# v's loads issued one a score step, the first duo read in 1024-byte pieces by two queues, the last bank emptied behind the first weights

## The chip, the core and the metric

The kernel runs on one core of one Trainium2 chip. TensorE (PE, with its weight loads as PEld), VectorE (DVE), ScalarE (ACT), GpSimd (POOL) and SyncE (SP) each work through a list of their own, in order, and wait for each other by semaphores. Matrix products land in PSUM banks, which DVE and ACT empty into SBUF. The metric is device time in microseconds of one execution.

## What is computed

Three stages stand behind each other: sigmoid attention over 4 batches of 12 heads (448 rows of 64), whose output is x of 1792 rows by 768, and then two mixtures of eight experts, each of which sends a row to one expert.

```python
scores = scale * np.matmul(q, k.transpose(0, 1, 3, 2)) - np.log(S)
attn_out = np.matmul(1.0 / (1.0 + np.exp(-scores)), v)
x = attn_out.transpose(0, 2, 1, 3).reshape(B * S, H * D)
# first mixture, for rows with x @ w_skip > 0; e_idx = argmax(x @ w_gate)
y[mask] = gate_w[mask, None] * (np.maximum(x[mask] @ w1[e], 0.0) @ w2[e])
# second mixture: e_idx = argmax of the normed x against normed expert rows, over tau
out[mask] = gate_w[mask, None] * (np.maximum(x[mask] @ w1[e], 0.0) @ w2[e])
```

## The kernel before

**Attention** (function `attention`) goes by duos: twelve groups of four heads, three to a batch. A duo has seven score steps, one for each 64 rows of k. In a step PE makes four products of 64x64 by 448 into a pair of banks `psS` (`score`, L589; the trace counts each as two matmuls), ACT turns the pair into `A` by one sigmoid (L593), and two steps later four products with v add into the two banks `psO` of the duo (`av`, L607). `psS` has two pairs, so the score of step h+2 waits for the sigmoid of step h. g counts steps over all duos; w is the duo and h the step in it.

**A duo's end** falls into step h=1 of the next duo: after the last `av`, `take_x` empties the two `psO` banks into `xT`, one on DVE (L524, two copies) and one on ACT (L522, two copies). At h=2 no `av` runs, at h=3 two do, the first of which needs the emptied banks.

**Loads.** `load_qk` reads k and q of the duo after next with eight DMAs of 112 KB on SP's queue, at h=0; `turn` transposes them on DVE (L580) at h=3 and h=4 of the duo before their use. `load_v` reads v of the next duo with four DMAs of 112 KB on ACT's queue, all at h=2, so on ACT they stand behind the two copies of `take_x` and ahead of the next sigmoid. Each DMA on SP's or ACT's queue takes the next of eight completion semaphores, and is issued only when the DMA that had it last has landed.

**The first duo** is read by `load_first` on SP with eight DMAs of 256-byte pieces, and `turn_first` transposes it on PE, four transposes of 112 rows by 128 columns for each of four halves (L572), into one bank each, emptied by DVE (L576) or ACT (L574).

**The steps beside attention.** A list of small steps runs one at a time beside the score steps. After a batch's last duo, router steps s1, s2 and s3 follow; each puts a few matmuls on PE. After the third batch (its last `av` is at h=1 of duo 9, and `at` counts steps from there) further steps follow by the table `at`: `gates` (two ACT operations, five on DVE, L336 to L340), `plan_first` (ten on DVE, L360 to L369, which write `pa`), `start` (reads `pa` into registers of ACT, DVE and SP, and loads the first weights), `gate_cols` (DVE, L347 to L678, which write `G`), `rows` (one product of `G` on PE into `ps_G`, L684), and seven steps of `split_gated` (ACT L697, DVE L695 and L698).

**Behind attention**, `split_unit` splits the first expert's weights into a high part h (ACT, L756) and a low part l (DVE, L757), and `dense` multiplies (L766 and L767 with h, L768 with l). The second of the two last `psO` banks is emptied between the first three pieces of this split and the rest; the first is emptied ahead of it.

Of the kernel before, what the change touches and what calls it, by code (L numbers as in the profile page):

```python
# [10 lines left out]
F32 = mybir.dt.float32  # L11
F32R = mybir.dt.float32r
I32 = mybir.dt.int32
AF = mybir.ActivationFunctionType
# [7 lines left out]
def sigmoid_attention_moe_moe_kernel(  # L22
# [15 lines left out]
    nc = tc.nc  # L38
    B, H, S, D = q.shape
    NE, DM, DF = w1.shape  # L40
    NT = B * S
    P = 112
    C = S // P
    NP = H // 2
# [20 lines left out]
    def bank(name):  # L65
        if not BANKS:
            return psA.tile([128, 512], F32, tag="psA", name=name)
        turn[0] ^= 1
        return BANKS[turn[0]]
# [10 lines left out]
    ident = const("ident", [128, 128])  # L80
    make_identity(nc, ident)
    bias = const("bias", [128, 1])
    nc.vector.memset(bias, 0.0)
    nc.scalar.activation(bias, bias, AF.Sigmoid)
    nc.vector.memset(bias, -math.log(S))
    xT = const("xT", [128, ND, NT])


# [437 lines left out]
    def attention():  # L526


        with ExitStack() as a:
# [5 lines left out]

            def load_first():

                t = LDU[0] = {nm: ld.tile([P, 2, C, 2 * D], F32, tag=nm + "0", name=nm + "0", bufs=1) for nm in "kq"}
                for i in range(2):
                    for nm, src in (("k", k), ("q", q)):  # L540
                        for j in range(2):
                            nc.sync.dma_start(
                                t[nm][:, i, :, j * D : (j + 1) * D], src[0, i + 2 * j].rearrange("(c p) d -> p c d", c=C)
                            )

            def load_qk(w):

# [7 lines left out]
                            src[b, h : h + 2, :, f : f + 32].rearrange("i (t r) d -> r (i t) d", r=32),  # L555
                        )

            def load_v(w):
                b, d = duos[w]
                t = LDU[w]["v"] = ld.tile([128, 2, NH, D], F32, tag="v", name="v")  # L560
                for i in range(2):
                    for j in range(2):
                        nc.scalar.dma_start(
                            t[KT * i : KT * i + KT, j], v[b, 4 * d + i + 2 * j].rearrange("(h r) d -> r h d", r=KT)
                        )

            def turn_first(nm, i):
                if i == 0:
                    ST[0, nm] = wk.tile([128, 2, S], F32, tag=nm + "T", name=nm + "T")
                ps = bank("ps_t")  # L570
                for c in range(C):
                    nc.tensor.transpose(ps[:, c * P : (c + 1) * P], LDU[0][nm][:, i, c], ident[:P, :P])  # L572
                if i:
                    nc.scalar.activation(ST[0, nm][:, i], ps[:, :S], AF.Copy)  # L574
                else:
                    nc.vector.tensor_copy(ST[0, nm][:, i], ps[:, :S])  # L576

            def turn(w, nm):
                dst = ST[w, nm] = wk.tile([128, 2, S], F32, tag=nm + "T", name=nm + "T")
# [16 lines left out]
            def av(w, h):  # L596
                t = LDU[w]["v"]
                b, d = duos[w]
                if h == 0:
                    ST[w, "o"] = [  # L600
                        bank("psO") if w == N - 1 and i else psO.tile([128, 512], F32, tag="psO", name="psO") for i in range(2)
                    ]
                at = ST.pop((w, "a", h))
                for i in range(2):
                    r = slice(KT * i, KT * i + KT)
                    for j in range(2):
                        nc.tensor.matmul(  # L607
                            ST[w, "o"][i][D * j : D * j + D, :S], lhsT=t[r, j, h, :], rhs=at[r, j, :],
                            start=h == 0, stop=h == NH - 1,
                        )  # L610
                if h == NH - 1:
                    for i in range(2):
                        if w < N - 1 or not i:
                            take_x(b, d, i, ST[w, "o"][i])

            N = len(duos)
            G, LAG = N * NH, 2
            load_first()
            load_v(0)
            for i in range(2):  # L620
                turn_first("k", i)
                turn_first("q", i)
            load_qk(1)
            load_v(1)
            load_qk(2)
            todo = setup_steps(wk)
            late = {}
            for g in range(G + LAG):
                w, h = divmod(g, NH)
                if 0 < w < N - 2 and h == 0:  # L630
                    load_qk(w + 2)
                if w > 0 and w + 1 < N and h == LAG:
                    load_v(w + 1)
                if g < G:
                    score(w, h)
                if w + 1 < N and h in (3, 4):
                    turn(w + 1, "kq"[h - 3])
                for r in {LAG: (), LAG + 1: (LAG + 1, LAG)}.get(h, (LAG,)):
# [6 lines left out]
                if done % NH == 0 and done > 0:  # L645
                    b, d = duos[done // NH - 1]
                    if d == NP // 2 - 1 and b < B - 1:
                        assert not todo
                        s1, s2, s3 = route_stages(R1, b, x_of(b))
                        todo = [None, s1, s2, None, s3]  # L650
                        if b == B - 2:
                            fs = [s1, s2, s3, lambda: gates(R1, 0, B - 1), lambda: plan_first(R1)] + first_steps()
                            at = [g + i for i in (2, 3, 5, 5, 7, 8, 8, 10, 10, 11, 14, 15, 16, 17)] + [G]
                            todo, late = [], schedule({}, fs, at)
            return ST[N - 1, "o"][1]

    R1, R2 = Route(0), Route(1)
    FIRST = {}
# [571 lines left out]
    NB = {}  # L1230
    for f in split_unit(0)[:3]:
        f()
    take_x(B - 1, NP // 2 - 1, 1, last_x)
    for f in split_unit(0)[3:]:
        f()
    na = nc.values_load(K["pa"][0:1, 0:1], min_val=0, max_val=1)
# [187 lines left out]
```

## Time and profile before

| what | us |
|---|---|
| median of three runs | 607.29 (606.9 to 608.69) |
| the profiled execution | 605.65 |
| its span, first to last instruction | 603.9 |
| PE busy in it | 572.8 |
| first score product on PE | 12.69 |
| first product with v | 18.66 |
| first expert product (L766) | 163.60 |

The profile is of one execution. Times in its views count from the span's start; 1.75 us of the execution lie outside the span. A row of the timeline gives start, duration, engine, line, operation, tiles and count; in brackets stands how long the engine was idle before it and what ended that. A q behind an engine's name means its queue or sequencer, as for the issue of a DMA.

### The profile page before, as it was taken

The page shows a single profiled execution, that of the slowest core. Times are in us where ns is not written, and L with a number is a line of the kernel's source. Part 1 is how long each engine was busy: PE and PEld are TensorE (multiplying, and loading weights), DVE is VectorE, ACT ScalarE, POOL GpSimd, SP SyncE. Part 2 cuts the span into 40 slices and gives each one's busy share as a digit, 9 for nine tenths or more (in the row PEclk, how much of TensorE's full clock was granted, in tenths as well). Part 3 has the DMA queues.
Part 4 walks back from the last instruction along what each step waited for, and adds up shares of the span by engine and source line. Part 5 has one row for each costly group of instructions (what it writes and reads, how often), then busy time and mean ns, then how long its engine had stood idle before and what let it go on. Part 6 is the DMA issues. An engine that isn't in the chain of part 4 may idle for free. (4 is left out here: it accounts for less than half of the span.)

```text
span 603.9 us, 9912 instructions
## 1 busy us (share of the span) xinstructions
PE 572.8 (95%) x3706; PEld 426.5 (71%) x3706; DVE 302.9 (50%) x762; ACT 274.3 (45%) x445; POOL 7.5 (1%) x15
## 2 busy tenths in 40 slices
PE   4999999999999999999969999999999999999994
PEld 2333334333389898997849899979998899898882
DVE  0452325237657679572147773577456674541222
ACT  1766675666932374342027423653248322532111
POOL 2010000000000000000000000000000000000000
PEclk9999999999999999999999999999999999999998
DMA  9989987963350504331538032260509050553343
GB/s 140 132 125 124 112 109 101 140 99 105 136 201 9 195 19 158 106 104 54 187 135 291 24 117 92 85 216 4 206 1 298 3 209 1 160 194 104 117 146 99
DMA packets 142618, 73.35 MB, mean 121 GB/s; under 512 B 107506, under 2 KB 132550, under 8 KB 142544
## 3 DMA queue, kind: packets, MB, share of 16 engines
q1 hardware_dynamic: 119616, 66.40, 43.1%
q10 hardware_dynamic: 22736, 5.97, 4.8%
q8 instruction: 38, 0.62, 0.4%
q14 instruction: 36, 0.29, 0.2%
q0 software_dynamic: 192, 0.07, 0.1%
HBM read 66.90 MB, written 5.70 MB: 120 GB/s over the span
## 5 line engine op out<-in xcount | busy, mean ns | idle before, releaser
L766 PE MATMUL bank<-xs,h 128*128 128x448 f32 x288 | 108.2, 376 | 5.7 <-DVEq L1268 5.0
L766 PE MATMUL y<-hh,h 128*128 128x448 f32 x288 | 108.5, 377 | 0.0
L786 ACT ACTIVATE hh<-bank 128x448 fp32r<-128x448 f32 x48 | 26.0, 542 | 178.7 <-PE bank L768 166.4
L768 PE MATMUL bank<-xs,l 128*128 128x448 f32 x288 | 105.6, 367 | 1.4 <-DVE l L757 1.4
L767 PE MATMUL bank<-xs,h 128*128 128x448 f32 x288 | 106.0, 368 | 0.0
L767 PE MATMUL y<-hl,h 128*128 128x448 f32 x288 | 105.6, 367 | 0.0
L768 PE MATMUL y<-hh,l 128*128 128x448 f32 x288 | 105.6, 367 | 0.0
L593 ACT ACTIVATE A<-psS,bias 128x896 f32<-128x896 f32 x84 | 83.5, 1006 | 46.5 <-PE psS L589 31.7
L757 DVE TENSOR_TENSOR l<-r,h 128x512 fp32r<-128x512 f32 (+1 forms) x115 | 85.3, 792 | 4.6 <-ACT h L756 3.0
L787 DVE SCALAR_TENSOR_TENSOR hl<-bank,hh 128x448 fp32r<-128x448 f32 x48 | 29.9, 623 | 114.5 <-ACT hh L786 114.1
L589 PE MATMUL psS<-qT,kT 64*64 64x448 f32 x672 | 79.6, 555 | 4.4 <-ACT A L593 4.3
L607 PE MATMUL psO<-A,v 64*64 64x448 f32 x672 | 78.0, 539 | 0.9 <-DVE xT L524 0.9
L756 ACT ACTIVATE h<-r 128x512 fp32r<-128x512 f32 (+1 forms) x115 | 74.6, 710 | 0.4 <-DMA r<-in_moe_w_dram 0.3
L766 PEld LDWEIGHTS bank<-xs,h 128*128 128x128 f32 x288 | 54.4, 189 | 15.2 <-issue 6.2
L766 PEld LDWEIGHTS y<-hh,h 128*128 128x128 f32 x288 | 54.1, 188 | 8.2 <-issue 2.9
L768 PEld LDWEIGHTS bank<-xs,l 128*128 128x128 f32 x288 | 54.4, 189 | 6.6 <-DVE l L757 1.7
L767 PEld LDWEIGHTS bank<-xs,h 128*128 128x128 f32 x288 | 54.5, 189 | 4.3
L768 PEld LDWEIGHTS y<-hh,l 128*128 128x128 f32 x288 | 54.1, 188 | 4.9
L767 PEld LDWEIGHTS y<-hl,h 128*128 128x128 f32 x288 | 54.2, 188 | 4.6 <-issue 0.2
L589 PEld LDWEIGHTS psS<-qT,kT 64*64 64x64 f32 x672 | 24.0, 135 | 45.2 <-issue 24.8
L607 PEld LDWEIGHTS psO<-A,v 64*64 64x64 f32 x672 | 28.7, 133 | 38.1 <-issue 27.5
L524 DVE COPY xT<-psO 64x448 f32<-64x448 f32 x24 | 14.8, 619 | 50.3 <-PE psO L607 50.1
(250 smaller groups left out, 444.3 us busy)
## 6 DMA issues: line engine op xcount, KB each, us to landing
r<-in_moe_w_dram SPq DMA_DIRECT2D x62, 768.0 KB, 6.0
k<-in_k_dram SPq DMA_DIRECT2D x48, 112.0 KB, 3.8
v<-in_v_dram ACTq DMA_DIRECT2D x48, 112.0 KB, 3.0
q<-in_q_dram SPq DMA_DIRECT2D x48, 112.0 KB, 3.9
out_dram<-row SPq DMA_DIRECT2D x3, 1344.0 KB, 6.7
out_dram<-row SPq DMA_DIRECT2D x1, 896.0 KB, 5.2
stg<-in_moe_w_dram SPq DMA_DIRECT2D x1, 768.0 KB, 7.3
row<-in_moe_w_dram SPq DMA_DIRECT2D x1, 768.0 KB, 8.8
```

Of the source, the lines that this page charges most:

```text
L524: nc.vector.tensor_copy(x, ps[64 * j : 64 * j + 64, :S])
L589: nc.tensor.matmul(ps[KT * i : KT * i + KT, j, :S], lhsT=kT[r, i, h * KT : (h + 1) * KT], rhs=qT[r, i], start=True, stop=True,)
L593: nc.scalar.activation(at, ps[:, :, :S], AF.Sigmoid, bias=bias, scale=1.0 / math.sqrt(D))
L607: nc.tensor.matmul(ST[w, "o"][i][D * j : D * j + D, :S], lhsT=t[r, j, h, :], rhs=at[r, j, :], start=h == 0, stop=h == NH - 1,)
L756: nc.scalar.activation(dst_h, src, AF.Copy)
L757: nc.vector.tensor_sub(dst_l, src, dst_h.bitcast(F32))
L766: nc.tensor.matmul(ps, lhsT=ah, rhs=bh, start=first, stop=False)
L767: nc.tensor.matmul(ps, lhsT=ah, rhs=bl, start=False, stop=False)
L768: nc.tensor.matmul(ps, lhsT=al, rhs=bh, start=False, stop=last)
L786: nc.scalar.activation(a, ps[:, :S], AF.Relu)
L787: nc.vector.scalar_tensor_tensor(l, ps[:, :S], 0.0, a.bitcast(F32), op0=ALU.max, op1=ALU.subtract)
```

## The change

- `load_v` takes a list of parts, and the loop calls it with one part a step, at h=2 to h=5, behind `score`. Duo 1's v, loaded ahead of the loop before, goes the same way in duo 0.
- `load_first` issues four DMAs of 224 KB instead of eight, k on SP and q on ACT, in pieces of 1024 bytes: a partition holds four rows in a row of the sequence (p c) instead of rows 112 apart (c p). `turn_first` makes eight transposes of 112 by 64 instead of four of 112 by 128 for each half, four to each bank of a `psS` pair, and both DVE and ACT empty one bank each, reordering the columns.
- The sigmoid on `bias`, which brings ACT's table load, and the memset behind it move from the kernel's head behind `load_first`.
- Both last `psO` banks are emptied behind the first three pieces of `split_unit`.
- The table `at` puts `gates` three steps later, `plan_first` one, `start` two, `gate_cols` three, and the others one or two later.

```diff
@@ const bias @@
     nc.vector.memset(bias, 0.0)
-    nc.scalar.activation(bias, bias, AF.Sigmoid)
-    nc.vector.memset(bias, -math.log(S))
@@ load_first @@
-                t = LDU[0] = {nm: ld.tile([P, 2, C, 2 * D], F32, tag=nm + "0", name=nm + "0", bufs=1) for nm in "kq"}
+                t = LDU[0] = {nm: ld.tile([P, 2, 2, C * D], F32, tag=nm + "0", name=nm + "0", bufs=1) for nm in "kq"}
                 for i in range(2):
-                    for nm, src in (("k", k), ("q", q)):
-                        for j in range(2):
-                            nc.sync.dma_start(
-                                t[nm][:, i, :, j * D : (j + 1) * D], src[0, i + 2 * j].rearrange("(c p) d -> p c d", c=C)
-                            )
+                    for nm, src, queue in (("k", k, nc.sync), ("q", q, nc.scalar)):
+                        queue.dma_start(
+                            t[nm][:, i], src[0, 0:4].rearrange("(j i) (p c) d -> p i j (c d)", i=2, c=C)[:, i]
+                        )
@@ load_v @@
-            def load_v(w):
+            def load_v(w, *parts):
                 b, d = duos[w]
-                t = LDU[w]["v"] = ld.tile([128, 2, NH, D], F32, tag="v", name="v")
-                for i in range(2):
-                    for j in range(2):
-                        nc.scalar.dma_start(
-                            t[KT * i : KT * i + KT, j], v[b, 4 * d + i + 2 * j].rearrange("(h r) d -> r h d", r=KT)
-                        )
+                if "v" not in LDU[w]:
+                    LDU[w]["v"] = ld.tile([128, 2, NH, D], F32, tag="v", name="v")
+                t = LDU[w]["v"]
+                for n in parts:
+                    i, j = divmod(n, 2)
+                    nc.scalar.dma_start(
+                        t[KT * i : KT * i + KT, j], v[b, 4 * d + i + 2 * j].rearrange("(h r) d -> r h d", r=KT)
+                    )
@@ turn_first @@
-                ps = bank("ps_t")
-                for c in range(C):
-                    nc.tensor.transpose(ps[:, c * P : (c + 1) * P], LDU[0][nm][:, i, c], ident[:P, :P])
-                if i:
-                    nc.scalar.activation(ST[0, nm][:, i], ps[:, :S], AF.Copy)
-                else:
-                    nc.vector.tensor_copy(ST[0, nm][:, i], ps[:, :S])
+                ps = psS.tile([128, 2, 512], F32, tag="psS", name="ps_t")
+                for j in range(2):
+                    for c in range(C):
+                        nc.tensor.transpose(
+                            ps[:D, j, c * P : (c + 1) * P], LDU[0][nm][:, i, j, c * D : (c + 1) * D], ident[:P, :P]
+                        )
+                    src = ps[:D, j, :S].rearrange("r (c p) -> r p c", c=C)
+                    dst = ST[0, nm][D * j : D * j + D, i].rearrange("r (p c) -> r p c", c=C)
+                    if j:
+                        nc.scalar.activation(dst, src, AF.Copy)
+                    else:
+                        nc.vector.tensor_copy(dst, src)
@@ av @@
-                        if w < N - 1 or not i:
+                        if w < N - 1:
@@ the loop @@
             load_first()
-            load_v(0)
+            nc.scalar.activation(bias, bias, AF.Sigmoid)
+            nc.vector.memset(bias, -math.log(S))
+            load_v(0, 0, 1, 2, 3)
...
             load_qk(1)
-            load_v(1)
             load_qk(2)
...
-                if w > 0 and w + 1 < N and h == LAG:
-                    load_v(w + 1)
                 if g < G:
                     score(w, h)
+                if w + 1 < N and 0 <= h - LAG < 4:
+                    load_v(w + 1, h - LAG)
...
-                            at = [g + i for i in (2, 3, 5, 5, 7, 8, 8, 10, 10, 11, 14, 15, 16, 17)] + [G]
+                            at = [g + i for i in (2, 3, 5, 8, 8, 10, 11, 12, 12, 13, 15, 16, 17, 18)] + [G]
...
-            return ST[N - 1, "o"][1]
+            return ST[N - 1, "o"]
@@ behind attention @@
-    take_x(B - 1, NP // 2 - 1, 1, last_x)
+    for i in range(2):
+        take_x(B - 1, NP // 2 - 1, i, last_x[i])
```

The next six pieces show the built order, with the semaphores that a row waits for (DMAHW are the eight of the DMAs, the other names are engines). On ACT, around a duo's end, before:

```order
L593 ACTIVATE A<-psS,bias 128x896 [waits PE_49,Activation_49] x4
L522 ACTIVATE xT<-psO 64x448 [waits PE_49]
L522 ACTIVATE xT<-psO 64x448
L563 DMA v<-in_v_dram 64x7x64 [waits DMAHW3_49,DMAHW2_49,DMAHW0_49]
L563 DMA v<-in_v_dram 64x7x64 [waits DMAHW3_49]
L563 DMA v<-in_v_dram 64x7x64 [waits DMAHW5_49]
L563 DMA v<-in_v_dram 64x7x64 [waits DMAHW6_49]
L593 ACTIVATE A<-psS,bias 128x896 [waits PE_49,Activation_49] x7
```

The same place on ACT with the change:

```order
L520 ACTIVATE xT<-psO 64x448 [waits PE_49]
L520 ACTIVATE xT<-psO 64x448
L597 ACTIVATE A<-psS,bias 128x896 [waits PE_49,Activation_49]
L562 DMA v<-in_v_dram 64x7x64 [waits DMAHW6_49,DMAHW7_49,DMAHW4_49,DMAHW1_49]
L597 ACTIVATE A<-psS,bias 128x896 [waits PE_49,Activation_49]
L562 DMA v<-in_v_dram 64x7x64 [waits DMAHW1_49]
L597 ACTIVATE A<-psS,bias 128x896 [waits PE_49,Activation_49]
L562 DMA v<-in_v_dram 64x7x64 [waits DMAHW3_49]
L597 ACTIVATE A<-psS,bias 128x896 [waits PE_49,Activation_49]
L562 DMA v<-in_v_dram 64x7x64 [waits DMAHW6_49]
```

The sigmoid now follows the two copies directly, and each DMA stands behind a sigmoid. On DVE, in duo 10 (the names are `pa`, the turned k and q of duo 11, and `G`), before:

```order
L368 TENSOR_REDUCE pl1r<-pl_1445 128x1 [waits DVE_49]
L369 CAST pa<-pl1r 128x3 [waits DVE_49]
L708 TENSOR_LOAD pa [waits DVE_49]
L347 ISA
L347 TENSOR_TENSOR dgt<-OH_98,PRIM_102 112x32
L350 TENSOR_REDUCE dg<-dgt 112x4 [waits DVE_49]
L351 ISA
L351 TENSOR_TENSOR dg<-dg,gr_334 112x4 [waits DVE_49]
L678 TENSOR_SCALAR G<-ident,dg 112x112 [waits DVE_49]
L678 TENSOR_SCALAR G<-ident,dg 112x112 x3
L580 STREAM_TRANSPOSE kT<-k 128x896 [waits DMAHW6_49,DMAHW7_49,DMAHW3_49,DMAHW0_49]
L580 STREAM_TRANSPOSE qT<-q 128x896 [waits DMAHW2_49,DMAHW3_49,DMAHW1_49,DMAHW0_49]
```

The same place on DVE with the change:

```order
L366 TENSOR_REDUCE pl1r<-pl_1470 128x1 [waits DVE_49]
L367 CAST pa<-pl1r 128x3 [waits DVE_49]
L584 STREAM_TRANSPOSE kT<-k 128x896 [waits DMAHW5_49,DMAHW7_49,DMAHW2_49,DMAHW0_49]
L584 STREAM_TRANSPOSE qT<-q 128x896 [waits DMAHW6_49,DMAHW7_49,DMAHW5_49,DMAHW4_49]
L713 TENSOR_LOAD pa [waits DVE_49]
L345 ISA
L345 TENSOR_TENSOR dgt<-OH_96,PRIM_100 112x32
L348 TENSOR_REDUCE dg<-dgt 112x4 [waits DVE_49]
L349 ISA
L349 TENSOR_TENSOR dg<-dg,gr_350 112x4 [waits DVE_49]
L683 TENSOR_SCALAR G<-ident,dg 112x112 [waits DVE_49]
L683 TENSOR_SCALAR G<-ident,dg 112x112 x3
```

The two stream transposes moved ahead of `gate_cols`; `gates` moved too, from ahead of the two copies of `take_x` to behind them. On PE, at the program's head, before:

```order
L572 MATMUL ps_t<-ident,k_129 128x112 [waits DMAHW1_49,DMAHW0_49,Pool_49]
L572 MATMUL ps_t<-ident,k_129 128x112 x3
L572 MATMUL ps_t<-ident,q_130 128x112 [waits DMAHW4_49,DMAHW2_49]
L572 MATMUL ps_t<-ident,q_130 128x112 x3
L572 MATMUL ps_t<-ident,k_129 128x112 [waits DMAHW7_49,DMAHW6_49,DVE_49]
```

The same place on PE with the change:

```order
L572 MATMUL ps_t<-ident,k_127 64x112 [waits DMAHW1_49,Pool_49]
L572 MATMUL ps_t<-ident,k_127 64x112 x3
L572 MATMUL ps_t<-ident,k_127 64x112 [waits DVE_49]
L572 MATMUL ps_t<-ident,k_127 64x112 x3
L572 MATMUL ps_t<-ident,q_128 64x112 [waits DMAHW0_49]
L572 MATMUL ps_t<-ident,q_128 64x112 x3
L572 MATMUL ps_t<-ident,q_128 64x112 [waits DVE_49]
```

Twice as many transposes stand there, and the second four of each half wait for DVE, which is its copy of the first four.

## Rows read from the trace of the kernel before

**Rows 1.** The page: PE busy, granted clock and rate in 40 slices.
```profile
PE 572.8 (95%) x3706; PEld 426.5 (71%) x3706; DVE 302.9 (50%) x762; ACT 274.3 (45%) x445; POOL 7.5 (1%) x15
PEclk9999999999999999999999999999999999999998
GB/s 140 132 125 124 112 109 101 140 99 105 136 201 9 195 19 158 106 104 54 187 135 291 24 117 92 85 216 4 206 1 298 3 209 1 160 194 104 117 146 99
```
**Rows 2.** Timeline of ACT, 77 to 92 us: start, duration, operation, count, idle before.
```profile
77.79 0.60 ACTq L563 DMA_DIRECT2D v<-in_v_dram  x1
78.02 0.54 ACT L522 ACTIVATE xT<-psO 64x448 f32<-64x448 f32 x1
...
80.55 1.91 ACT L593 ACTIVATE A<-psS,bias 128x896 f32<-128x896 f32 x2 [1.44 <-issue]
...
84.22 1.01 ACT L593 ACTIVATE A<-psS,bias 128x896 f32<-128x896 f32 x1 [0.50 <-PE psS L589]
85.72 1.01 ACT L593 ACTIVATE A<-psS,bias 128x896 f32<-128x896 f32 x1 [0.50 <-PE psS L589]
```
**Rows 3.** Timeline of PE, the same duo end.
```profile
78.95 1.93 PE L607 MATMUL psO<-A,v 64*64 64x448 f32 x16
81.61 0.98 PE L589 MATMUL psS<-qT,kT 64*64 64x448 f32 x8 [0.73 <-ACT A L593]
```
**Rows 4.** Timeline of PE, a duo end that a router step follows.
```profile
53.28 1.92 PE L607 MATMUL psO<-A,v 64*64 64x448 f32 x16
55.13 1.70 PE L235 MATMUL ps_r<-xT,wr 128*32 128x448 f32 x12
```
**Rows 5.** Timeline of PE, duos 10 and 11.
```profile
143.07 1.83 PE L607 MATMUL psO<-A,v 64*64 64x448 f32 x16 [0.87 <-DVE xT L524]
...
147.04 1.02 PE L684 MATMUL ps_G<-G,one 112*128 112x448 f32 x2 [0.61 <-DVE G L678]
...
155.60 1.73 PE L607 MATMUL psO<-A,v 64*64 64x448 f32 x16
157.43 0.98 PE L589 MATMUL psS<-qT,kT 64*64 64x448 f32 x8
```
**Rows 6.** Timeline of DVE, duo 10.
```profile
140.11 0.75 DVE L336 RECIPROCAL ge<-ge 112x96 f32<-112x96 f32 x1
...
145.47 0.22 DVE L347 TENSOR_TENSOR dgt<-OH,PRIM 112x32 f32 x1 [0.83 <-DVE pa L369]
...
146.90 1.10 DVE L580 STREAM_TRANSPOSE kT<-k 128x896 f32<-128x896 f32 x1
```
**Rows 7.** Timeline of all engines where attention ends.
```profile
163.71 1.27 DVE L524 COPY xT<-psO 64x448 f32<-64x448 f32 x2
...
164.90 3.62 DVE L757 TENSOR_TENSOR l<-r,h 128x512 fp32r<-128x512 f32 x5
...
165.63 0.47 PE L768 MATMUL bank<-xs,l 128*128 128x448 f32 x1 [1.35 <-DVE l L757]
```
**Rows 8.** Timeline of all engines, from the span's start.
```profile
5.20 0.98 PE L572 MATMUL ps_t<-ident,k 112*128 112x112 f32 x4 [5.20 <-DMA k<-in_k_dram]
6.22 0.62 DVE L576 COPY kT<-ps_t 128x448 f32<-128x448 f32 x1 [3.86 <-PE ps_t L572]
...
12.80 0.54 ACT L574 ACTIVATE qT<-ps_t 128x448 f32<-128x448 f32 x1 [1.02 <-PE ps_t L572]
```
**Rows 9.** PE's groups to 14 us: count, then busy us, mean ns, idle before.
```profile
L572 PE MATMUL ps_t<-ident,k 112*128 112x112 f32 x8 | 2.0, 399 | 6.8 <-DMA k<-in_k_dram 6.8
```
**Rows 10.** PE's groups between 12 and 16.5 us, same columns.
```profile
L589 PE MATMUL psS<-qT,kT 64*64 64x448 f32 x16 | 4.0, 964 | 0.0
```
**Rows 11.** Issue to landing: of the first duo's DMAs (L542).
```profile
DMA to landing us min/median/max: 2.2/5.2/6.4
```
**Rows 12.** The same of the v DMAs (L563), 30 to 150 us.
```profile
DMA to landing us min/median/max: 2.6/3.0/4.1
```
**Rows 13.** The same of the k and q DMAs (L553), 34 to 140 us.
```profile
DMA to landing us min/median/max: 2.5/3.8/5.0
```

## The prediction

> **What bounds the kernel now.** I read the page first: PE is busy 95% of the span [rows 1], so a gain has to come from PE's idle spots or from its slow stretches, and the question is which of them the change touches. Then I followed PE through attention (12.7 to 163.6 us) in the timeline. In the middle of a duo, ACT sets the beat together with PE: its sigmoids take 1.01 and start 1.50 apart, each waiting 0.50 for PE [rows 2], so there PE has no pause and ACT has 0.49 to spare. PE pauses at the duos' ends. At a plain end two `av` start at 78.95 and the next score at 81.61, 2.66 later, with a wait for `A` in between [rows 3]; the same two `av` at the end that has no v DMAs (into duo 11) take 157.43 - 155.60 = 1.83, of which 1.73 is their own span [rows 5]. ACT shows why: the sigmoid that the score waits for stood idle 1.44 for "issue" behind the two copies, while ACT's queue issued v's DMAs at 0.60 each [rows 2]. The other touched spots are duo 10 [rows 5, 6], attention's end [rows 7] and the start [rows 8]. Behind 163.6 us PE multiplies without a stop that the change touches, so what attention gains or loses goes through to the end.
>
> **v's DMAs, one a step.** Four issues of 0.60, 2.4 and more, overlap the two copies (0.54 each) and leave 1.44 idle. Without them the sigmoid starts at 80.55 - 1.44 = 79.11 and ends at 80.12, before the two `av` are through. These I put at 1.55 (followed by a router step, two of them take 55.13 - 53.28 = 1.85 with some stall left [rows 4]; a step of score and `av` is 1.50, so two `av` can't be much above that). So each plain end gains 2.66 - 1.55 = **1.11**. There are six of them: into duos 1, 2, 4, 5, 7 and 8, **6.66** in sum (lower bound, with 1.83 for the two `av`: 5.0). Into duos 3, 6 and 9 a router step of PE already fills most of the hole; there 1.85 - 1.55 = 0.30 each, **0.9** (bounds 0 and 3.3). The moved issues go behind the sigmoids of h=2 to h=5. An issue is on ACT's queue, and the first row of rows 2 shows that it runs on while ACT computes (77.79 to 78.39 beside the copy from 78.02). Beside a sigmoid of 1.01 in a step of 1.50, 0.60 costs nothing; were it to run behind the sigmoid, the step would be 1.61 or more (the fourth rival). The data come later, but not late: the last part is issued at h=5, some 4 steps of 1.50 ahead of its first use, and the slowest v DMA landed 4.1 after its issue [rows 12].
>
> **Duo 10.** Before, it lost 0.87 (two `av` wait for DVE's copies, which stood behind `gates`) and 0.61 (the product into `ps_G` waits for `G`) [rows 5], and about 0.5 of the v stall beyond the 0.87 (between 0.24 and 1.11): 2.0. With the change `gates`, `plan_first`, both stream transposes and `gate_cols` stand in this order on DVE. `gates` and `plan_first` took 145.47 - 140.11 = 5.36 less 1.27 for the copies (the price of two in rows 7) and less 0.83 idle [rows 6]: 3.3. The transposes are two at 1.10: 2.2. `gate_cols` is 146.90 - 145.47 = 1.43. Together 6.9. On the clock of the end in rows 2, the chain begins when the sigmoid of h=2 has ended (80.12) and ACT's two small operations for `gates` are through, for which I allow 0.7: 80.8. It ends at 87.7. PE comes to the `ps_G` product at h=6: two `av` to 80.50, three steps of 1.50, 85.0. So PE waits 2.7 there instead of 2.0 in three places: **0.7 lost** (bounds: 0.5 gained if the chain starts 1.2 earlier, 1.0 lost). Into duo 11 `split_gated`'s ACT part no longer stands ahead of the sigmoid: 1.83 - 1.55, **0.3** gained.
>
> **The last bank.** DVE's `L757` starts at 164.90, behind the two copies of 1.27, and PE's first product with l waits 1.35 for it [rows 7]. With the copies behind the first three pieces it starts at 163.71: **1.19** gained. The copies then end about 167, and nothing but a later router step reads that bank.
>
> **The start.** Four transposes take 0.98, one 0.40 [rows 8, 9], so starts are 0.19 apart and eight in a row take 1.76. With the change the second four of each half wait for DVE's copy of the first four (the order shows it): 0.62 [rows 8] and 0.09 for two handovers. PE's chain is 0.98 + 4 x 0.71 + 3 x 1.76 + 0.98 = 10.1, and with ACT's last copy (0.54, and 0.05) 10.7. Before, the same was 12.80 + 0.54 - 5.20 = 8.1 [rows 8], in which PE waited for data. When can it begin? The first DMA of 112 KB landed 2.2 after issue at best and 6.4 at worst [rows 11], and PE began at 5.20. The new first k and q are 448 KB; the first 112 KB at 2.2, the other 336 KB at the best rate of rows 1 (298 GB/s) 1.1, the first issue at about 0.7: **4.0** (bounds: 2.9, with 2.2 alone, and 5.9, with the median 5.2). So q and k are turned at 14.7 instead of 13.34. Against that, three score products instead of one can be done before the last copy; behind it stood 15 of 16, which took 18.66 - 13.34 = 5.3, or 0.35 each, so two less are 0.7. Net **0.7 lost** (bounds: 0.5 gained, 2.6 lost). The moved sigmoid on `bias` lies in the wait for data.
>
> The Trainium skill ("DMA: Bandwidth & Descriptors", section "Issuing engines are not separate DMA queues") speaks against the two queues: DMAs of different issuing engines end up on the same 16 engines, and what is saved is only the sequencer's time to issue. By that q on ACT's queue saves about one issue and the start would be 4.6, my sum 0.6 lower; no row here shows two queues reading at once with nothing else under way, so this stays open until the landings of the changed kernel.
>
> **The sum.** 6.66 + 0.9 - 0.7 + 0.3 + 1.19 - 0.7 = 7.65. The profiled execution was 605.65, so 598.0 for its like; the median 607.29 is 0.3% above it, which makes **599.6**.
>
> **The rivals.**
> - *The denser start ends PE's slow stretch sooner.* The first score products run slow: 964 ns each in the records [rows 10] and 5.3 us for thirty records, where eight take 0.98 in a plain step [rows 3]. At the plain rate the thirty would be 3.7. The clock row prints 9 (the 2.4 GHz level) from the first slice on [rows 1], although PE had done nothing to 5.20, so it doesn't say when this ended. If the eight groups with pauses of 0.71, in place of four with waits of up to 1.55, bring full rate before the scores, 1.6 comes off there and up to 1.6 off the later transposes; I take 2.5 together: **597.1**. For it: less idle time. Against: the pauses remain. The Trainium skill ("TensorE: Matmul & The Clock Gate", Part 1) says that the clock starts throttled and is released by sustained activity, which goes with this rival; the granted clock that this trace prints doesn't show it.
> - *The start comes late.* If 224 KB pieces land like the median of the 112 KB ones, 5.2 after issue, PE begins at 5.9, and 1.9 more is lost: **601.5**. For it: the landings of 2.2 to 6.4. Against: the pieces are larger and fewer.
> - *The issue isn't hidden beside the sigmoid,* so that the change moves the cost and doesn't remove it. Then a step with a DMA takes 1.01 + 0.64 = 1.65 instead of 1.50, four steps in ten duos: 6.0 lost, **605.6**. Against it: the overlap in rows 2.
> - *A stall of ACT behind a DMA semaphore* (slower). A DMA is issued only when the one that had its semaphore eight before has landed, and SP and ACT share the eight. The fourth v DMA of a duo then hangs on a k or q DMA of SP, which in turn hangs on a v DMA of the duo before. This ring gives two landings and two issues a duo for 14.3 us, a duo's 10.6 and the 3.75 of the two and a half steps between. At the rows' medians (3.0 and 3.8, [rows 12, 13]) it needs 7.8, at the maxima 10.1. It decides from a mean landing of 6.7 and eats the whole gain at 7.1; at 8.0 each of nine duos would lose 2.6 more than gained by the even beat, **623**. Against it: no landing above 5.0.
>
> **How the numbers follow.** The forecast 0.52, the faster start 0.20, the late start 0.13, the issue not hidden 0.10, the stall 0.05. The range 594.5 to 603.0 holds the first three with their bounds (597.1 less 2.6, 601.5 and 1.5) and leaves out the last two. 0.3% is about what can be told from no change, 1.8 us: faster 0.85 and half of the not hidden issue, 0.90; same 0.05; slower 0.05.
>
> **What would show it.** On ACT at plain ends, no 1.44 for "issue" behind the copies, and the sigmoid directly behind them; on PE there, 1.55 from the two `av` to the next score. In duo 10, no wait of `av` for `xT`, and one of 2.7 before `ps_G`. At the end of attention, `L757` at the start of the split, and the first product with l waiting 0.2. At the start, the second transposes of each half waiting on DVE, the first transposes at 4.0, the first product with v 0.7 later than 18.66. Steps of 1.65 at h=2 to h=5 would show that the issues aren't hidden; an ACT wait ahead of v's DMAs would show the ring. The prediction is wrong if ends other than these held the time, if two `av` can't go in 1.55, or if the start differs by more than 2.6.

## The result

| | before | changed |
|---|---|---|
| median of four runs each | 607.99 us (606.9 to 608.86) | 601.50 us (601.29 to 602.25) |
| the profiled execution | 605.65 | 602.25 |
| its span | 603.9 | 600.5 |
| first product with v on PE | 18.66 | 20.05 |
| first expert product | 163.60 | 161.31 |
| first product with l | 165.63 | 162.25 |

The ratio is 0.9896, with a 95% interval of 0.9875 to 0.9918: the changed kernel is faster by 5.0 to 7.6 us. Forecast were 599.6 and a range of 594.5 to 603.0. The two profiled executions differ by 3.4 only; most of the rest comes out in the experiments.

At a plain duo end the stall is gone. On ACT of the changed kernel (timeline; start, us, operation) the sigmoid now follows the two copies directly, and the first v DMA runs on the queue beside the copies, which answers to [rows 2]:

```profile
76.53 1.09 ACT L520 ACTIVATE xT<-psO 64x448 f32<-64x448 f32 x2
77.10 0.60 ACTq L562 DMA_DIRECT2D v<-in_v_dram  x1
77.64 1.01 ACT L597 ACTIVATE A<-psS,bias 128x896 f32<-128x896 f32 x1
77.83 0.60 ACTq L562 DMA_DIRECT2D v<-in_v_dram  x1
```

PE's timeline of the changed kernel, in the order of [rows 3, 4, 5, 7]: a plain end, an end with a router step, duo 10, and the first product with l:

```profile
77.36 2.03 PE L611 MATMUL psO<-A,v 64*64 64x448 f32 x16
78.86 1.28 PE L593 MATMUL psS<-qT,kT 64*64 64x448 f32 x8
...
88.12 2.03 PE L611 MATMUL psO<-A,v 64*64 64x448 f32 x16
90.08 1.70 PE L233 MATMUL ps_r<-xT,wr 128*32 128x448 f32 x12
...
146.39 1.02 PE L689 MATMUL ps_G<-G,one 112*128 112x448 f32 x2 [2.05 <-DVE G L683]
147.34 1.55 PE L593 MATMUL psS<-qT,kT 64*64 64x448 f32 x8
148.64 1.74 PE L611 MATMUL psO<-A,v 64*64 64x448 f32 x8
...
162.25 0.47 PE L773 MATMUL bank<-xs,l 128*128 128x448 f32 x1 [0.26 <-DVE l L762]
```

From two `av` to the next score it is 78.86 - 77.36 = 1.50 where it was 2.66. At the router's end it is 1.96 where it was 1.85. In duo 10 PE waits 2.05 for `G`, and what follows is slow: from the score at 147.34 to its `av` it is 1.30, where a plain step has 0.75. The view by stretches of the same kernel shows it; each row gives the stretch, its length, the busy time of PE, PEld, DVE, ACT and POOL, and in its last three columns the granted clock, the DMA share and GB/s:

```profile
143.90:146.40 2.50, 0.45 (x7) 0.01 (x1) 2.33 (x9) 1.03 (x2) 0.00 (x0) 1.00 0.45 93
146.40:148.60 2.20, 2.20 (x10) 0.76 (x14) 0.58 (x2) 0.54 (x1) 0.00 (x0) 0.78 1.02 324
148.60:150.10 1.50, 1.50 (x12) 0.54 (x8) 0.58 (x2) 1.10 (x2) 0.00 (x0) 0.50 1.03 386
150.10:152.10 2.00, 2.00 (x22) 0.82 (x17) 0.63 (x1) 0.82 (x2) 0.00 (x0) 0.76 1.05 377
```

PE was busy 0.45 of 2.50 ahead, and then the granted clock went to 0.50 (the 1.2 GHz level) and came back. It cost 2.20 x 0.22 + 1.50 x 0.50 + 2.00 x 0.24 = 1.7.

The start of the changed kernel (PE, DVE and ACT), which answers to [rows 8]:

```profile
4.56 0.93 PE L572 MATMUL ps_t<-ident,k 112*64 112x112 f32 x4 [4.56 <-DMA k<-in_k_dram]
5.52 0.62 DVE L580 COPY kT<-ps_t 64x448 f32<-64x448 f32 x1 [2.19 <-PE ps_t L572]
6.19 0.96 PE L572 MATMUL ps_t<-ident,k 112*64 112x112 f32 x4 [0.71 <-DVE kT L580]
...
14.42 0.54 ACT L578 ACTIVATE qT<-ps_t 64x448 f32<-64x448 f32 x1 [1.88 <-PE ps_t L572]
```

Four times PE waits 0.71 for DVE's copy, and PE begins at 4.56, but the last copy ends only at 14.96.

Going from the two `av` of one duo to those of the next gives the account between the two profiles. Six plain ends gave 0.92, 1.09, 1.07, 0.99, 0.81 and 0.97, 5.85 together; the first two router ends lost 0.2; duo 10, with the third router end ahead of it, lost 2.3; duo 11 gave 0.32; the first product with l waits 1.09 less; the start lost 1.39. The sum is 3.4, the difference of the spans.

### The profile page after: what moved, and what is told of

Same layout as the page of the kernel before. It is cut to its first block, busy times and chain, and to the rows that moved or that the text cites. A ratio compares the mean times of both kernels' runs of the same rounds, so it can differ in the third digit from the quotient of the medians.

```text
span 600.5 us, 9949 instructions
## 1 busy us (share of the span) xinstructions
PE 575.3 (96%) x3722; PEld 441.7 (74%) x3722; DVE 304.2 (51%) x764; ACT 274.9 (46%) x447; POOL 7.5 (1%) x15
## 5 line engine op out<-in xcount | busy, mean ns | idle before, releaser
L593 PE MATMUL psS<-qT,kT 64*64 64x448 f32 x672 | 88.7, 557 | 0.3 <-ACT A L597 0.3
L611 PE MATMUL psO<-A,v 64*64 64x448 f32 x672 | 87.1, 544 | 0.0
L611 PEld LDWEIGHTS psO<-A,v 64*64 64x64 f32 x672 | 35.1, 134 | 32.9 <-issue 20.6
L593 PEld LDWEIGHTS psS<-qT,kT 64*64 64x64 f32 x672 | 32.9, 136 | 32.2 <-issue 18.1
```

What stands on the lines that cost most here:

```text
L593: nc.tensor.matmul(ps[KT * i : KT * i + KT, j, :S], lhsT=kT[r, i, h * KT : (h + 1) * KT], rhs=qT[r, i], start=True, stop=True,)
L611: nc.tensor.matmul(ST[w, "o"][i][D * j : D * j + D, :S], lhsT=t[r, j, h, :], rhs=at[r, j, :], start=h == 0, stop=h == NH - 1,)
```

## The experiments

Three sets were run; the runs of a set share a chip and the runs of the kernel before on it. Ratios are to those, formed round by round, so they differ a little from the quotient of two medians. The third set, on another chip, holds the second profile of the kernel before, the old order at the last banks and the two runs under "The start once more".

### The change once more, and its parts

**The change again.**

> The changed kernel once more, as the measure for the others of this set. It was 601.5 against 608.0, but the two profiled executions differ by 3.4 only (605.65 and 602.25). If the executions of one kernel scatter by about 1, the ratio comes out between 0.988 and 0.992 again. If the gain were the 3.4 of the two profiles, it would be 0.9944.

It took 601.61 (600.24 to 602.16) against 607.40, ratio 0.9895 [0.9877, 0.9913]. The profiled execution took 602.16, nearly what the first one took, but differs in two places. In duo 10 PE waited just as long for `G`, and its clock did not fall (PE's timeline):

```profile
146.81 1.02 PE L689 MATMUL ps_G<-G,one 112*128 112x448 f32 x2 [2.05 <-DVE G L683]
147.76 0.98 PE L593 MATMUL psS<-qT,kT 64*64 64x448 f32 x8
```

The score behind the wait takes 0.98 instead of 1.55, and duos 9 and 10 took 28.08 instead of 29.76. The fall of the clock in duo 10 is thus a matter of the execution, not of the kernel alone: of the six profiles in this study with a wait of 2.05 there, four show it (this change's first one, the old order at the last banks, the banks of their own and the first run with transposes of the identity) and two do not (this one and the old start). The second place is far behind attention, at the start of the second mixture. There PE waits some 5 us, in all kernels of this study, and the granted clock falls behind it. In the stretch from 290 to 330 us it was, in this run,

```profile
290.00:330.00 40.00, 35.45 (x178) 28.32 (x177) 20.35 (x29) 16.74 (x32) 0.00 (x0) 0.91 0.57 200
```

and in the first profile of the changed kernel

```profile
290.00:330.00 40.00, 35.05 (x183) 28.00 (x182) 20.15 (x29) 16.44 (x32) 0.00 (x0) 0.96 0.57 200
```

0.91 and 0.96 of 40 us are 3.6 and 1.6 us of clock. That scatter, of about 2 us, is larger than several of the terms that I had summed.

**The kernel before again,** for the same stretch.

> The kernel before once more, for a second profile. Theory: its first profiled execution (605.65) was 1.7 below the median of its timed ones because the stretch of half the granted clock at the start of the second mixture was short in it (it cost about 1.7 where others of this study show 3.4); an execution near 607.4 shows it longer, and the same times as the first profile everywhere ahead of it. Rival (the executions differ in attention): the first expert product is not at 163.6 but 1 or more later.

It took 606.98. Its first expert product is at 163.49 and that of the first profile at 163.60; its plain ends, duo 10 and start are the same within 0.2. The stretch differs: first the kernel before in its first profile, then in this one.

```profile
290.00:330.00 40.00, 35.03 (x183) 27.98 (x182) 18.07 (x29) 14.59 (x28) 0.00 (x0) 0.96 0.56 198
```
```profile
290.00:330.00 40.00, 35.25 (x180) 28.11 (x179) 17.84 (x29) 13.86 (x26) 0.00 (x0) 0.91 0.55 194
```

So the theory holds: the first profile of the kernel before was one with the short fall. Executions of a kind are to be compared: 606.98 and 602.16 (on two chips), both with 0.91 there and none in duo 10, differ by 4.8; 605.65 and 602.25, both with 0.96, but the second with a fall in duo 10, by 3.4. The medians differ by 5.8 and 6.5 in the two sets. The last 1 us or more of this was not found in a profile.

**v's DMAs alone.** The kernel before with `load_v` by parts, as in the change, and this edit in the loop:

```diff
-                if w > 0 and w + 1 < N and h == LAG:
-                    load_v(w + 1)
                 if g < G:
                     score(w, h)
+                if w + 1 < N and 0 <= h - LAG < 4:
+                    load_v(w + 1, h - LAG)
```

> The kernel before with v's DMAs issued one a step and nothing else. Theory: this is the whole gain of attention: 0.98 at each of six plain ends, nothing at the router ends, some 0.5 in duo 10: 6.4 below the kernel before, about 601.6, as fast as the whole change, since the rest of the change loses as much as it gains. Rival (the other parts carry gain of their own, so that each is worth having): 603 or more.

602.31 (600.51 to 602.58), ratio 0.9911 [0.9893, 0.9928]. That is most of the change's gain, as the theory has it, but the 0.5 expected in duo 10 came as a loss: the duos from 9 on take 34.0 where they took 33.1 before. The next run shows the same loss.

**The old table.** The changed kernel with this line:

```diff
-                            at = [g + i for i in (2, 3, 5, 8, 8, 10, 11, 12, 12, 13, 15, 16, 17, 18)] + [G]
+                            at = [g + i for i in (2, 3, 5, 5, 7, 8, 8, 10, 10, 11, 14, 15, 16, 17)] + [G]
```

> The changed kernel with the table of steps of the kernel before. Theory: the wait of 2.05 for G in duo 10 goes, and with it the stretch of half the granted clock behind it; the wait of 0.87 for DVE's copies and one of about 0.6 for G come back: 2.3 to 2.8 faster than the changed kernel, about 599. The granted clock stays full in duo 10. Rival (the new table pays: the slow stretch has another cause, such as the weights' DMAs that begin in it): slow stretch and time stay, 601.5.

601.93 (600.71 to 603.20), ratio 0.9901 [0.9881, 0.9921]; the changed kernel had 601.61 beside it. The expected 2.3 to 2.8 did not come. The waits for the copies (0.87) and for `G` (0.63) came back as foreseen, but a third one came with them. PE's timeline:

```profile
151.65 0.98 PE L611 MATMUL psO<-A,v 64*64 64x448 f32 x6
153.02 1.34 PE L611 MATMUL psO<-A,v 64*64 64x448 f32 x9 [0.39 <-DMA v<-in_v_dram]
```

Duo 11's first `av` waits for v. The view of the v DMAs' line in duo 10 of this kernel ends with

```profile
DMA to landing us min/median/max: 2.6/4.2/7.8
```

and the DMAs of the same stretch in the changed kernel (issues: KB each, median us to landing) are

```profile
r<-in_moe_w_dram SPq DMA_DIRECT2D x4, 768.0 KB, 7.2
v<-in_v_dram ACTq DMA_DIRECT2D x4, 112.0 KB, 2.6
```

With the old table the four weight DMAs of `start` are issued before v's fourth part, which landed 7.8 after its issue. With the new one they are issued behind it, and v landed in 2.6. So the table and the spread of v belong together: spread over four steps, v's last part would otherwise stand behind 3 MB of weights. Duos 9 to 11 took 33.9 with the old table and, with the new, 33.4 without a fall of the clock and 35.1 with one, which is why the runs can't tell them apart. The Trainium skill ("DMA: Bandwidth & Descriptors", section "Issuing engines are not separate DMA queues") says that DMAs of different issuing engines run on the same 16 engines and interleave; v on ACT's queue behind weights on SP's, 7.8 instead of 2.6, agrees with it.

**The old start.** The changed kernel with `load_first` and `turn_first` of the kernel before; the lines show the first of the two.

```diff
-                    for nm, src, queue in (("k", k, nc.sync), ("q", q, nc.scalar)):
-                        queue.dma_start(
-                            t[nm][:, i], src[0, 0:4].rearrange("(j i) (p c) d -> p i j (c d)", i=2, c=C)[:, i]
-                        )
+                    for nm, src in (("k", k), ("q", q)):
+                        for j in range(2):
+                            nc.sync.dma_start(
+                                t[nm][:, i, :, j * D : (j + 1) * D], src[0, i + 2 * j].rearrange("(c p) d -> p c d", c=C)
+                            )
...
```

> The changed kernel with the first duo's loading and turning of the kernel before. Theory: the first product with v comes 1.4 earlier (at 18.7 instead of 20.05) and the execution is 1.4 faster, about 600.1. Rival (the later start is taken up by a wait later in duo 0 or 1): no difference.

600.43 (599.33 to 602.14), ratio 0.9880 [0.9860, 0.9901], 1.2 under the median of the changed kernel beside it, though the intervals overlap; the first product with v came at 19.26 instead of 20.46, and all duos behind it were as long as in the changed kernel within 0.3. The new start costs about what it shows.

**The old order at the last banks.** The changed kernel with the first of the two emptied inside attention again:

```diff
-                        if w < N - 1:
+                        if w < N - 1 or not i:
                             take_x(b, d, i, ST[w, "o"][i])
-    for i in range(2):
-        take_x(B - 1, NP // 2 - 1, i, last_x[i])
+    take_x(B - 1, NP // 2 - 1, 1, last_x[1])
```

> The changed kernel with the first of the last two banks emptied ahead of the split's first pieces, as before. Theory: PE's first product with l waits 1.3 again instead of 0.3, 1.1 slower than the changed kernel, 602.6. Rival (PE makes the time up, since the next weights or the router step wait for something else): 601.5.

602.80 (601.90 to 604.96), ratio 0.9912 [0.9892, 0.9933]; the changed kernel had 0.9896 and 0.9895 in other sets. On PE:

```profile
163.93 0.47 PE L773 MATMUL bank<-xs,l 128*128 128x448 f32 x1 [1.37 <-DVE l L762]
```

The wait is back at 1.37 from 0.26, as before the change [rows 7]; the difference of the ratios, 1.0 us, has its size, though the intervals overlap.

### What the two new losses hang on

**Banks of their own at the start.** The changed kernel, in `turn_first`:

```diff
-                ps = psS.tile([128, 2, 512], F32, tag="psS", name="ps_t")
                 for j in range(2):
+                    ps = psO.tile([128, 512], F32, tag="psO", name="ps_t") if j else bank("ps_t")
...
```

> The changed kernel, with the two groups of four transposes of each half written into two PSUM tiles of their own instead of the two banks of one pair. Theory: the second group no longer waits 0.71 for DVE's copy of the first, four times: the last transposes end 2.8 earlier, and the first product with v starts near 17.4 instead of 20.1 to 20.5; about 2.8 faster than the changed kernel, 598.8. Rival (the start is bound by data: k and q of the second half landed 6.0 and 6.5 after the start, later than PE wants them): the first product with v moves by less than 1.

595.73 (594.85 to 596.35), ratio 0.9804 [0.9789, 0.9819], nearly 6 under the median of the changed kernel (5.5 by the ratios) and twice what was expected. PE's start in it:

```profile
4.85 1.67 PE L572 MATMUL ps_t<-ident,k 112*64 112x112 f32 x8 [4.85 <-POOL pc_i L102]
6.32 1.70 PE L572 MATMUL ps_t<-ident,q 112*64 112x112 f32 x8
7.82 1.58 PE L572 MATMUL ps_t<-ident,k 112*64 112x112 f32 x8
9.23 0.93 PE L572 MATMUL ps_t<-ident,q 112*64 112x112 f32 x8
10.09 2.41 PE L593 MATMUL psS<-qT,kT 64*64 64x448 f32 x16
12.84 1.88 PE L593 MATMUL psS<-qT,kT 64*64 64x448 f32 x16 [0.34 <-ACT A L597]
14.55 1.68 PE L611 MATMUL psO<-A,v 64*64 64x448 f32 x16
```

The first product with v is at 14.55 instead of 20.05, 5.5 earlier. Of this, the four waits of 0.71 are 2.8. The other 2.7 are speed: the fourth group of eight takes 0.93 where the first took 1.67, and the scores behind it run nearly at the plain rate. The groups of PE over the start show the same, first of the changed kernel, then of this one (count, busy us, mean ns):

```profile
L593 PE MATMUL psS<-qT,kT 64*64 64x448 f32 x32 | 5.6, 758 | 0.3 <-ACT A L597 0.3
```
```profile
L593 PE MATMUL psS<-qT,kT 64*64 64x448 f32 x32 | 4.3, 555 | 0.3 <-ACT A L597 0.3
```

This is the first rival of the prediction, which in the change itself did not happen, because the pauses of 0.71 stayed. With PE working from 4.85 without a pause, PE doubles its rate before 9.3 (in the last run below, whose start is the same, near 10: its fourth group takes 1.42); with a pause of 0.71 behind every 1.7 of work it did not do so before the scores. The granted clock prints 1.00 from 0 to 20 us in both kernels, so it can't be read for the first stretch of a run; that the doubling is one of the clock is read from the durations alone. The Trainium skill ("TensorE: Matmul & The Clock Gate", Part 1) has the clock start throttled and sustained activity release it; these durations agree.

**Transposes of the identity ahead.** The changed kernel with

```diff
+            ps = psS.tile([128, 2, 512], F32, tag="psS", name="warm")
+            for c in range(13):
+                nc.tensor.transpose(ps[:, 0, :128], ident, ident)
             for i in range(2):
                 turn_first("k", i)
```

> The changed kernel with 13 transposes of the identity on PE ahead of the first real ones, into a bank that nobody reads, while PE waits for the first k. Theory: the first transposes (0.39 each) and the first score products run slow because PE begins at the lower of its two clock levels, and work ahead of them ends that sooner: transposes 0.2 each, the chain of transposes 3 shorter, the score products 1.4 shorter, first product with v near 16, 4 faster, about 597.5. Rival (they are slow for another reason, as data that land at the same time or waits for copies): no difference.

601.55 (595.72 to 602.58), ratio 0.9888 [0.9854, 0.9922]. The profiled execution took 601.45 and shows no gain at the start:

```profile
1.35 3.04 PE L628 MATMUL warm<-ident 128*128 128x128 f32 x13 [1.35 <-POOL ident masks.py:199]
4.68 0.95 PE L572 MATMUL ps_t<-ident,k 112*64 112x112 f32 x4 [0.29 <-DMA k<-in_k_dram]
6.35 0.95 PE L572 MATMUL ps_t<-ident,k 112*64 112x112 f32 x4 [0.71 <-DVE kT L580]
```

The expectation fell: after work from 1.35 to 4.39, followed by the pauses as they were, the transposes took as long as before, and the first product with v came at 19.91, where it was at 20.05 and 20.46. One execution of the six took 595.72, which is what a fast start would give; it was not profiled, so this is a guess.

**The turns of duo 11 ahead of `gates`.** The changed kernel with

```diff
-                if w + 1 < N and h in (3, 4):
-                    turn(w + 1, "kq"[h - 3])
+                first = 1 if w == N - 2 else 3
+                if w + 1 < N and h in (first, first + 1):
+                    turn(w + 1, "kq"[h - first])
...
-                            at = [g + i for i in (2, 3, 5, 8, 8, 10, 11, 12, 12, 13, 15, 16, 17, 18)] + [G]
+                            at = [g + i for i in (2, 3, 5, 8, 8, 11, 11, 13, 13, 14, 15, 16, 17, 18)] + [G]
```

> The changed kernel with the two stream transposes of duo 11 at h=1 and h=2 of duo 10, ahead of gates on DVE, and start, gate_cols and the product into ps_G one step later. Theory: G is ready about 145 counted as in the changed kernel, one step before PE comes to its product; the wait of 2.05 in duo 10 goes, no fall of the granted clock behind it can come, and v still lands ahead of the weights: duos 9 to 11 take 31.4 together instead of 33.4 to 35.1; 2.0 to 3.7 faster, about 599. Rival (another wait takes the place, of a sigmoid for pa or of duo 11's first score for k and q): less than 0.7 gained.

599.92 (598.47 to 600.35), ratio 0.9869 [0.9852, 0.9885]. In the profile PE's wait for `G` is gone, at the price of 0.31 for a copy that stands behind the first turn:

```profile
138.42 1.83 PE L611 MATMUL psO<-A,v 64*64 64x448 f32 x16 [0.31 <-DVE xT L522]
...
146.20 1.02 PE L690 MATMUL ps_G<-G,one 112*128 112x448 f32 x2
```

Duos 9 to 11 took 31.96, 1.4 less than in the changed kernel without a fall and 3.1 less than with one. The time is some 1.6 lower by the ratios.

**The three together.**

> The three edits of this set together on the changed kernel. Theory: they lie at different places and add up, less what the shorter start leaves for the transposes ahead of it to save: 7 to 9 faster than the changed kernel, about 593 to 595. Rival (the start is bound by data once the transposes are fast): 596.

593.87 (592.93 to 594.43), ratio 0.9782 [0.9769, 0.9796]; 7.7 under the median of the changed kernel (6.9 by the ratios). The first product with v came at 14.93, no earlier than with the banks alone.

### The start once more

**No pause behind the identity.** As the last, with 15 transposes of the identity.

> The three edits together, with 15 transposes of the identity ahead of the first real one instead of 13, so that they reach to the landing of the first k and PE has no pause of 0.47 between. Theory: what counts for the rise of PE's clock is work without a pause; with the pause the real transposes began at the lower level again and rose near 10, without it the rise comes during the first transposes, and the first product with v near 12.5 to 13 instead of 14.9: 2 faster, about 591.8. Rival (the rise waits for a fixed time after the first real work or after the launch): no difference, 593.9.

593.54 (593.14 to 594.67), ratio 0.9768 [0.9744, 0.9792]. On PE:

```profile
5.02 1.70 PE L572 MATMUL ps_t<-ident,k 112*64 112x112 f32 x8 [0.20 <-DMA k<-in_k_dram]
6.52 1.40 PE L572 MATMUL ps_t<-ident,q 112*64 112x112 f32 x8
7.75 0.55 PE L572 MATMUL ps_t<-ident,k 112*64 112x112 f32 x4
8.68 0.57 PE L572 MATMUL ps_t<-ident,k 112*64 112x112 f32 x4 [0.38 <-ACT kT L578]
```

In this one profile the rate doubles earlier, near 7, as the theory said, but the expected 2 us did not come: PE now waits 0.38 for ACT's copy out of a bank that it needs again, and the first product with v is at 14.40. ACT's copy seems to be late behind v's DMAs, as the sigmoid was at the duos' ends before the change (ACT's timeline):

```profile
5.52 2.52 ACTq L562 DMA_DIRECT2D v<-in_v_dram  x2
8.09 0.54 ACT L578 ACTIVATE kT<-ps_t 64x448 f32<-64x448 f32 x1 [4.88 <-PE ps_t L572]
```

The products that it copies were through by 6.72, but two of v's first DMAs stand ahead of it on ACT, the second of which was issued at 7.4. In all four kernels with banks of their own, ACT's first copy starts 0.04 to 0.05 behind the end of these issues. No run moved them away.

**Without the identity.**

> The same without any transposes of the identity. Theory: with the pause they did nothing, so this is as fast as the three together, 593.9, its first product with v at 14.6. Rival (they shortened the slow stretch a little): 595 or more.

593.36 (592.33 to 594.41), ratio 0.9758 [0.9735, 0.9782]. The transposes of the identity gave nothing that the times show. This version, the changed kernel with banks of their own and the early turns, is some 14 us faster than the kernel before and some 8 than the changed one, with two edits.

## Why the prediction was right, and where not

**v's DMAs.** The mechanism was right, in each of its rows. The two `av` take 1.50 to 1.55 to the next score, and no sigmoid waits for "issue" behind the copies. Over the steady part of attention the view of waits (us in total, times, longest) lists for the kernel before

```profile
ACT A L593 <- issue: 11.5, 8, 1.5
PE psS L589 <- ACT A L593: 3.6, 5, 0.7
```

and for the changed one neither, but one for PE's weight loads that the kernel before doesn't have:

```profile
PEld psO L611 <- ACT xT L520: 0.8, 5, 0.2
```

The issues of 0.60 cost nothing beside a sigmoid: steps stayed at 1.50, so the rival of the issue that isn't hidden is out, and between 30 and 150 us v's landings grew to at most 5.8 without a stall of ACT ahead of a v DMA, so the rival of the stall is out. The term was mis-sized: 5.85 at the six plain ends, 0.98 each, instead of 6.66. The step that failed is the assumption that nothing else is late there. The pair of `av` starts 1.58 to 1.86 behind the two scores ahead of it at five of nine ends, where it was 1.52 or 1.53 before, and at the same five ends the weight loads of `av` wait for ACT's copy of the second bank, 0.2 at a time. That this wait is the whole of the missing 0.81 was not tested.

**The router ends.** The 0.9 was wrong: the first two lost 0.2, and the third lies in the account of duo 10. I had read the 0.30 beyond 1.55 [rows 4] as a rest of the v stall. It is still there without it (1.96), so it goes with the router step itself, whose first weight load stands 0.70 behind "issue" in both kernels.

**Duo 10.** The sum for DVE's chain held. It was 6.9, and in the changed kernel it runs from 139.47 to 146.33, 6.86 (DVE's timeline, first and last operation):

```profile
139.47 0.75 DVE L334 RECIPROCAL ge<-ge 112x96 f32<-112x96 f32 x1 [1.61 <-ACT ge L333]
145.49 0.84 DVE L683 TENSOR_SCALAR G<-ident,dg 112x112 f32<-112x112 f32 x4
```

PE waited 2.05 where 2.7 was foreseen, since the chain began 0.3 earlier than forecast and PE came 0.4 later. Duos 9 and 10 together lost 0.59 in the run without a fall of the clock, where 0.7 was forecast for duo 10 and a gain of 0.3 for the router end. What the prediction did not have is the fall, 1.7 more in some executions. Nor did it see what the move of `start` is good for. I had costed the table by DVE's chain alone, and counted v's landing at 4.1 at most; behind the weights it is 7.8, and the old table would have brought that with the spread.

**Duo 11 and the last bank.** 0.32 for 0.3 forecast, and 1.09 for 1.19: both right.

**The start.** 1.39 lost in place of 0.7, 1.8 in the second run. The first transposes began at 4.56 (forecast 4.0), the chain from there to the last copy took 10.4 (10.7), and the first product with v came 5.1 behind it (4.6). Two terms were mis-sized: the landing (the first 224 KB of k took 3.7 from issue, not 3.3, with q's landing beside them) and what stands between the last copy and the first product with v. Whether two queues bring the data sooner than one is not settled by this, since PE is bound by its own waits behind 4.56; its start there is nearer to the 4.6 that the prediction gave for no gain from two queues than to its 4.0, but in the profiles of this study with the same loads it lies between 4.56 and 5.03. The price of the first rival was about right, 2.5 against the 2.7 that the run with banks of their own gained in speed. Its 3.7 for thirty scores at the plain rate was too long, though: it counts 0.98 for eight, which holds the end of the last one, and from start to start eight take 0.75 (a step of 1.50 holds two eights), so thirty take about 2.8.

**The sum.** Forecast 7.65, between like executions 4.8, in medians 5.8 to 6.5. Some two thirds of the missing 2.85 is at v (0.81 at the plain ends and 1.1 at the router's), and 0.7 to 1.1 at the start. That the time still fell into the range is in part luck: a loss at the router ends and a fall of the clock in duo 10 lie outside the bounds that the range was made of. The scaling of the profile to the median, 0.3%, hid a cause, at least in part: the profiled execution of the kernel before was a short one by the clock of the second mixture.

## What to carry to other kernels

DMA issues on a computing engine's queue were free here one at a time beside a long operation, and four in a row between two of them held the next one up by 1.44; but when loads are spread later, look at what else is issued on any queue by then, and move that too. A wait on the bounding engine costs more than its length when the clock falls behind it, and pauses of 0.7 at the start cost about as much again in PE's rate (2.7 beside 2.8): ask of each pair of PSUM banks whether the next writer waits for the reader of its neighbour. Before a profile is scaled to a median, look whether the profiled execution was one of the short ones.

## What the runs showed that was not expected

- The same kernel has executions with and without a fall of the granted clock behind the same wait of 2.05, and falls of two lengths behind the wait at the start of the second mixture (0.96 and 0.91 over 40 us). The mean granted clocks of the runs of the kernel before, 0.989 to 0.992, are worth about 1.8 us of their scatter (2.2 to 4.7 us in a set); the rest was not found.
- PE's rate at the start doubled after work without a pause from 4.85 to about 9.2 in one profile and from 4.98 to about 10 in another, and not under pauses of 0.71, with the granted clock printed as 1.00 all along.
- A 112 KB DMA on one queue landed in 2.6 when it was issued ahead of four DMAs of 768 KB on another, and in 7.8 when issued behind them.
